# The last chunk's tail: another order of the sums, earlier stores, a separate buffer for the transposed rows, one bank copied by ScalarE

## The chip, the core and the metric

The kernel runs on one core of a Trainium2 chip. A core has TensorE (PE, matmuls into PSUM), VectorE (DVE), ScalarE (ACT) and GpSimd (POOL) for elementwise work, and SyncE (SP), which here only issues DMAs. The metric is the device time in microseconds (us); the median of several runs counts. Profiles are of one execution each.

## The reference

An FNet mixing step, then a gated feed-forward block with a sigmoid gate, in float32:

```python
X = np.fft.fft(x, axis=1)            # x: 8 x 3008 x 256
X = np.fft.fft(X, axis=2)
x2 = X.real.reshape(8 * 3008, 256)
gate = 1.0 / (1.0 + np.exp(-(x2 @ w_gate)))   # 256 x 1536
val = x2 @ w_val                              # 256 x 1536
out = (gate * val) @ w_out                    # 1536 x 256
```

The real part of a Fourier transform of real input has a symmetry: row k and row 3008 - k are made from the same two products, once with a plus and once with a minus between them. The kernel computes both rows of such a pair together; below they are called the rows k and the mirrored rows.

## The kernel before

**Tiling.** There are 8 batches. In each, the 1505 rows k are cut into six chunks, five of 252 and the last of 246. A chunk goes through the 1536 features in 12 steps of 128 features, so the main loop (line 749) has 8 x 6 x 12 = 576 iterations. An iteration does, for its 128 features: `front_a` and `front_b` (eight matmuls in the trace, into a PSUM bank called `pf`), `gate_a` and `gate_b` (two sigmoids on ScalarE and three elementwise instructions on VectorE, which give the gated values `h`), and one third of `back` for an earlier group of three steps.

**The product with w_out.** `back` (line 567) multiplies three steps' `h` with blocks of `w_out`, as a fast matrix multiplication with 15 products: 17 blocks of sums of `h` (made by GpSimd, `H_SUMS`, buffer `sf`) against 15 blocks of `w_out`. The 15 products lie in five PSUM banks `po0` to `po4`, three in a bank, and are added up over the chunk's four groups. In the fourth group, when a bank is complete, it is copied (line 584) to the SBUF tile `c`, in which product i lies at columns i*R to (i+1)*R, with R = 168, or 164 in chunks of 246. The last chunk of all doesn't copy bank 4: its products 12 to 14 are read from PSUM.

**The sums.** `finish` (line 591) combines the 15 products into the output with the list `C_SUMS` (line 66). An entry `((dst, a, b, op), e)` sets product dst to a + b or a - b. With e = 1 the entry goes to GpSimd, but in the last chunk alone; in all others every sum is VectorE's. When all is done, rows 3, 4, 5 of `c` hold one half of the output features and rows 12, 13, 14 the other (`OUT = (3, 12)`). The first n columns of each half (products 3, 4 and 12, 13) belong to the rows k, the next n (products 4, 5 and 13, 14) to the mirrored rows. `flip(s, h)` (line 610) transposes one of these four pieces on VectorE into the tile `os` (s = 0: rows k, s = 1: mirrored rows, h: which half), and `store(s)` (line 617) issues eight DMAs of it: for each of four groups of partitions one of 56 KB and one of the rest, 5 to 7 KB. In the last chunk these alternate between SP's and ScalarE's queues; otherwise all are SP's. The tile `os` has one buffer.

**What sets the order.** The order of instructions on every engine is the order in which the program issues them. In all chunks but the last, `finish` doesn't do its work at once: it appends each sum, flip and flip-with-store to the list `later`, and each iteration of the main loop takes two or three items from it (line 767: two in even iterations, three in odd ones). What is left of the list after iteration 575 is done behind the last `gate_b` (line 774), ahead of the last matmuls' copies. In the last chunk, `finish` does everything at once.

A chunk's list has 24 items: 14 sums (up to the one that sets product 5), `flip(0, 0)`, `flip(1, 0)`, six sums, then `flip(0, 1)` with `store(0)`, and `flip(1, 1)` with `store(1)`. Each DMA also waits until the DMA that had its completion semaphore before it is done; there are eight of these semaphores for the DMAs of SP and ScalarE, used in turn.

Of the kernel before, what the change touches and what calls it, by code (L numbers as in the profile page):

```python
# [7 lines left out]
F32 = mybir.dt.float32  # L8
# [54 lines left out]
            (10, 10), (14, 1), (15, 7), (16, 14))  # L63
PLACE = (0, 1, 2, 5, 3, 4, 6, 7, 8, 9, 10, 11, 14, 13, 12)

C_SUMS = (((8, 1, 8, 0), 0), ((1, 1, 0, 0), 0), ((3, 3, 1, 0), 0), ((1, 6, 2, 0), 1), ((0, 0, 10, 1), 0),
          ((11, 0, 11, 0), 1), ((4, 4, 0, 1), 0), ((4, 4, 1, 0), 0), ((11, 11, 5, 0), 1),
          ((9, 9, 8, 0), 1), ((10, 14, 8, 1), 0), ((7, 7, 10, 0), 0), ((6, 11, 6, 0), 1),
          ((5, 5, 7, 1), 0), ((9, 13, 9, 1), 0), ((9, 9, 2, 0), 0), ((14, 9, 14, 0), 0),
          ((13, 13, 6, 1), 0), ((12, 9, 12, 0), 0), ((12, 11, 12, 1), 0))  # L70
OUT = (3, 12)
HUGE = float((2 ** 24 - 1 - 2 ** 20) * 2.0 ** -7)

# [2 lines left out]
def kernel(  # L76
# [10 lines left out]
    nc = tc.nc  # L87
    B, _, _, _, D = xf.shape
    F = moe_w_gate.shape[1]
    P = 128  # L90
    S = out.shape[0] // B
    M = S // 2
    NK = M + 1
# [5 lines left out]
    CH = 252  # L99
    NB = 1 + max(b // 3 for b in PLACE)  # L100
    WC = 256
    HD = D // 2
    TB = 32
# [16 lines left out]
    sp = ctx.enter_context(tc.tile_pool(name="sp", bufs=2))  # L120
    cp = ctx.enter_context(tc.tile_pool(name="cp", bufs=2))
    op = ctx.enter_context(tc.tile_pool(name="op", bufs=1))
# [3 lines left out]
    def mm(o, l, r, start, stop):  # L126
        nc.tensor.matmul(o, l, r, start=start, stop=stop, skip_group_check=True)  # L127
# [370 lines left out]
    def seed(i):  # L498


        _, _, n, f, _ = cut(i)
        PF[i] = bank("pf").rearrange("p (g n) -> p g n", g=2)[:, :, 0:n]
        for g in range(2 if i >= NFT else 0):
            nc.scalar.activation(PF[i][:, g], EK[i // NFT], AF.Copy, scale=ge[:, g, f : f + 1])  # L504

    def front_a(i):
        (pk, *_), ks, _, _, fs = cut(i)
        if i < NFT:
            seed(i)
        for g in range(2):  # L510
            mm(PF[i][:, g], G1[:, g, fs], pk[:, ks], i < NFT and g == 0, True)

    def part(i):

        pqe, ks, n, f, _ = cut(i)
        AP[i] = app.tile([P, 2, CH], F32, name="ae", tag="ae")[:, :, 0:n]
        if i >= NFT:
            nc.scalar.activation(AP[i], PF[i], AF.Copy, scale=2.0)  # L518
            return
        for g in range(2):  # L520
            nc.vector.scalar_tensor_tensor(out=AP[i][:, g], in0=pqe[2][:, ks],  # L521
                                           scalar=ge[:, g, f : f + 1], in1=PF[i][:, g],
                                           op0=ALU.mult, op1=ALU.add)

    def front_b(i):
        (_, qk, *_), ks, _, _, fs = cut(i)
        for g in range(2):
            mm(PF[i][:, g], G2[:, g, fs], qk[:, ks], False, True)

    def gate_a(i):  # L530

        n = cut(i)[2]
        p, fh = i // 3, i % 3
        z = Z[i] = zp.tile([P, 2, CH], F32, name="z", tag="z")[:, :, 0:n]
        if fh == 0:
            H[p] = hp.tile([P, 3, 2 * WC], F32, name="h", tag="h")[:, :, 0 : 2 * n]
        nc.scalar.activation(H[p][:, fh, 0:n], PF[i][:, 0], AF.Sigmoid)  # L537
        if i < NFT:
            nc.vector.scalar_tensor_tensor(out=z[:, :, ::-1], in0=AP.pop(i), scalar=2.0, in1=PF[i],  # L539
                                           op0=ALU.mult, op1=ALU.subtract)  # L540
        else:
            nc.vector.tensor_tensor(z[:, :, ::-1], AP.pop(i), PF[i], op=ALU.subtract)  # L542

    def block(p, i):

        R = 2 * chunks[groups[p][1]][1] // 3
        return H[p][:, i % 3, i // 3 * R : (i // 3 + 1) * R] if i < 9 else SF[p][:, i - 9, 0:R]
# [16 lines left out]
    later = []  # L564
    C = {}

    def back(p, part):

        b, c, g = groups[p]
        n = chunks[c][1]  # L570
        R = 2 * n // 3
        last = p == len(groups) - 1
        if part == 0 and g == 0:
            PO[:] = [pso.tile([P, 2 * WC], F32, name=f"po{t}", tag=f"po{t}") for t in range(NB)]
        for at_, (hb, wb) in list(enumerate(PRODUCTS))[part * 5 : part * 5 + 5]:
            t, j = divmod(PLACE[at_], 3)
            mm(PO[t][:, j * R : (j + 1) * R], wf[:, g, wb], block(p, hb), g == 0 and at_ % 3 == 0,
               g == NG - 1)
            if g == NG - 1 and at_ % 3 == 2:
                if t == 0:  # L580
                    C[0] = cp.tile([P, 10 * WC], F32, name="c", tag="c")
                    nc.gpsimd.memset(C[0][:, 15 * R : 15 * R + 40], 0.0)
                if not (last and t == NB - 1):
                    (nc.vector.tensor_copy if t % 2 else nc.scalar.copy)(
                        C[0][:, 3 * t * R : 3 * (t + 1) * R], PO[t][:, 0 : 3 * R])
        if part == 2:
            del H[p], SF[p]
            if g == NG - 1:
                finish(b, c, last)

    def finish(b, c, last):
        k0, n = chunks[c]
        R = 2 * n // 3
        more = k0 + n > NK
        nb = -(-n // TB)
        t = C.pop(0)
        queues = (nc.sync, nc.scalar) if last else (nc.sync,)
        os_ = []

        new = set()  # L600

        def sum_(dst, a, b, op, engine=nc.vector):

            there = lambda i: last and i >= 3 * (NB - 1) and i not in new
            v = [PO[NB - 1][:, (i - 3 * NB + 3) * R : (i - 3 * NB + 4) * R] if there(i) else
                 t[:, i * R : (i + 1) * R] for i in (a, b)]
            engine.tensor_tensor(t[:, dst * R : (dst + 1) * R], *v, op=(ALU.subtract, ALU.add)[op])  # L607
            new.add(dst)

        def flip(s, h):  # L610
            if not os_:
                os_.append(op.tile([P, NK + 1], F32, name="os", tag="os")[:, 0 : 4 * WC].rearrange(
                    "p (s b h j) -> p s b h j", s=2, h=2, j=TB))
            c0 = OUT[h] * R + (n + more if s else 0)
            nc.vector.transpose(os_[0][:, s, 0:nb, h, :], t[:, c0 : c0 + nb * TB])

        def store(s):
            m, r0 = (min(n, M - k0), b * S + k0) if s == 0 else (
                n - (k0 == 0) - more, b * S + S - k0 - n + 1 + more)
            full = m // TB  # L620
            for a in range(4):
                ps = slice(a * TB, (a + 1) * TB)
                cs = slice(a * 2 * TB, (a + 1) * 2 * TB)
                queues[a % len(queues)].dma_start(
                    out=out[r0 : r0 + full * TB, cs].rearrange("(b t) d -> t b d", t=TB),
                    in_=os_[0][ps, s, 0:full].rearrange("p b h j -> p b (h j)"))
                if m > full * TB:
                    queues[a % len(queues)].dma_start(out=out[r0 + full * TB : r0 + m, cs],
                                      in_=os_[0][a * TB : a * TB + m - full * TB, s, full].rearrange(
                                          "p h j -> p (h j)"))  # L630

        def add(f):
            if last:
                f()
            else:
                later.append(f)
        for x, e in C_SUMS:
            add(lambda x=x, e=e: sum_(*x, engine=(nc.vector, nc.gpsimd)[last and e]))
            if x[0] == 5:
                add(lambda: flip(0, 0))  # L640
                add(lambda: flip(1, 0))
        for half in range(2):
            add(lambda half=half: (flip(half, 1), store(half)))

# [60 lines left out]
    for j in range(3, len(jobs)):  # L707
        w, c = jobs[j]
        i = (0, 1, 4, 7, 9, 10)[c] if w == 2 else 2 * c - 3 + w
# [4 lines left out]
    count = 3 * len(groups)  # L714
# [34 lines left out]
    for i in range(count):  # L749
        front_a(i)  # L750
        if i < NFT:
            part(i)
        if i:
            gate_a(i - 1)
        if i >= NFT:
            part(i)
        if i0 <= i + 1 < count:
            seed(i + 1)
        if i:
            gate_b(i - 1)  # L760
        todo = pre.pop(i, []) + use.pop(i, [])
        for f in [parts_.pop(0)] + todo if parts_ else todo + [lambda: parts_ and parts_.pop(0)()]:
            f()
        if i >= 5:
            back((i - 5) // 3, (i - 5) % 3)
        front_b(i)
        for f in later[0 : 2 + i % 2]:
            f()
        del later[0 : 2 + i % 2]
        for f in side.pop(i, []):  # L770
            f()
    gate_a(count - 1)
# [3 lines left out]
    for i in range(count, count + 5):  # L776
        back((i - 5) // 3, (i - 5) % 3)
# [49 lines left out]
```

## Time and profile before

| what | value |
|---|---|
| median of three runs | 1982.71 us (1982.51 to 1985.28) |
| the profiled execution, its own time | 1985.11 us |
| its span, first to last instruction | 1983.2 us |
| mean granted TensorE clock | 0.993 |
| PE busy | 1936.4 us, 98% of the span |
| DVE, ACT, POOL busy | 1488.3, 1338.3, 1624.8 us |
| last matmul ends | 1968.73 us |

Times inside the profile are counted from the first instruction. Lines of the profile give start, duration, engine, line of the kernel, operation and tiles; what stands in brackets is the time for which the engine was idle before, and what ended it. `SPq` and `ACTq` are DMA issues on the queues of SP and ScalarE. A group of several instructions of one kind is merged into one row with its count. A TensorE at 98% busy doesn't mean that it works at its peak, but that there is next to nothing between its matmuls.

### The profile page before, as it was taken

Reading aid. Unit: us, or ns where it says so; the run is one execution under the profiler, and the core shown is the slowest. Engines: PE = TensorE matmul, PEld = TensorE weight load, DVE = VectorE, ACT = ScalarE, POOL = GpSimd, SP = SyncE. Lnnn points to the kernel's source line nnn. Section 1 sums busy time; section 2 is a strip of 40 time slices with the busy share of each in tenths; the row PEclk is TensorE's granted clock in tenths of the full one; section 3 lists DMA queues with packets and bytes.
Section 4 is the critical chain, followed back from the end, with each engine's and each line's share of the span. In section 5 each row is a group of like instructions: output and inputs, shape, how many; then the busy total and the mean of one; then the engine's idle time right before and its main releaser. Section 6 shows DMA issues by size and latency. Waiting matters only on the chain.

```text
span 1983.2 us, 34391 instructions
## 1 busy us (share of the span) xinstructions
PE 1936.4 (98%) x11232; PEld 1790.2 (90%) x11232; DVE 1488.3 (75%) x3179; ACT 1338.3 (67%) x3102; POOL 1624.8 (82%) x2857
## 2 busy tenths in 40 slices
PE   6899999999999999999999999999999999999997
PEld 4689889998999899998999989999899989999996
DVE  7788777886787677786778867787678777777776
ACT  3467667675777667775777757777577766777774
POOL 3879898997889878997889868998688886777775
PEclk8999999999999999999999999999999999999999
DMA  8353423212112120222013121221210110011001
GB/s 266 88 132 85 124 50 104 51 22 78 18 46 54 19 77 14 54 50 77 15 21 78 20 77 20 45 54 20 77 22 14 18 23 14 14 18 23 14 16 30
DMA packets 171444, 101.41 MB, mean 51 GB/s; under 512 B 133890, under 2 KB 163204, under 8 KB 168588
## 3 DMA queue, kind: packets, MB, share of 16 engines
q1 hardware_dynamic: 169294, 98.64, 20.3%
q8 instruction: 90, 1.47, 0.3%
q10 hardware_dynamic: 1940, 0.56, 0.1%
q14 instruction: 88, 0.72, 0.1%
q0 software_dynamic: 32, 0.00, 0.0%
HBM read 74.45 MB, written 50.18 MB: 63 GB/s over the span
## 4 chain that ended last, share of the span: by engine, by line
PE 94%; DMA 2%; DVE 2%; POOL 1%; ACT 1%; issue 0%; SPq 0%; ACTq 0%; DVEq 0%; POOLq 0%
PE pf L127 48%; PE po L127 41%; PE ev L127 4%; DMA ge<-G 1%; DMA st<-in_stab_dram 1%; PE od L127 1%; PE ps L127 0%; DVE wf L315 0%; DMA wx<-in_moe_w_val_dram 0%; DVE ae L521 0%; POOL sf L560 0%; POOL wf L315 0%; DVE z L539 0%; DMA raw<-in_moe_w_gate_dram 0%; DMA wx<-in_moe_w_gate_dram 0%
## 5 line engine op out<-in xcount | busy, mean ns | idle before, releaser
L560 POOL TENSOR_TENSOR sf<-h 128x168 f32<-128x168 f32 (+1 forms) x960 | 550.8, 592 | 233.1 <-DVE h L556 233.0
L560 POOL TENSOR_TENSOR sf<-h,sf 128x168 f32<-128x168 f32 (+1 forms) x1152 | 646.1, 581 | 54.2 <-DVE h L556 54.2
L127 PE MATMUL pf<-qk,G 128*128 128x252 f32 (+1 forms) x2304 | 582.7, 376 | 3.8 <-DVE ae L521 1.9
L127 PE MATMUL pf<-pk,G 128*128 128x252 f32 (+1 forms) x2304 | 583.0, 376 | 0.0
L556 DVE TENSOR_TENSOR h<-z 128x252 f32<-128x252 f32 (+1 forms) x576 | 293.7, 510 | 377.0 <-ACT z L555 376.4
L504 ACT ACTIVATE pf<-ek,ge 128x252 f32<-128x252 f32 (+1 forms) x1128 | 531.4, 471 | 18.4
L127 PE MATMUL po<-sf,wf 128*128 128x168 f32 (+1 forms) x3072 | 530.4, 306 | 0.0
L518 ACT ACTIVATE ae<-pf 128x504 f32<-128x504 f32 (+1 forms) x564 | 332.6, 590 | 240.1 <-PE pf L127 239.3
L127 PEld LDWEIGHTS pf<-pk,G 128*128 128x128 f32 x2304 | 436.3, 190 | 53.1 <-issue 2.3
L127 PEld LDWEIGHTS po<-sf,wf 128*128 128x128 f32 x3072 | 473.3, 190 | 8.4
L127 PE MATMUL po<-h,wf 128*128 128x168 f32 (+1 forms) x2688 | 475.9, 306 | 2.1 <-ACT a L471 1.6
L607 DVE TENSOR_TENSOR c<-c 128x168 f32<-128x168 f32 (+1 forms) x950 | 467.1, 514 | 8.5
L127 PEld LDWEIGHTS po<-h,wf 128*128 128x128 f32 x2688 | 427.5, 190 | 19.2 <-ACT a L471 2.0
L127 PEld LDWEIGHTS pf<-qk,G 128*128 128x128 f32 x2304 | 409.9, 190 | 30.7 <-DVE ae L521 2.9
L542 DVE TENSOR_TENSOR z<-ae,pf 128x504 f32<-128x504 f32 (+1 forms) x564 | 372.4, 660 | 19.1 <-ACT h L537 18.8
L537 ACT ACTIVATE h<-pf 128x252 f32<-128x252 f32 (+1 forms) x576 | 218.7, 380 | 172.3 <-PE pf L127 160.2
L555 ACT ACTIVATE z<-z 128x252 f32<-128x252 f32 (+1 forms) x576 | 230.8, 401 | 76.7 <-DVE z L542 46.5
L554 DVE TENSOR_TENSOR h<-h,pf 128x252 f32<-128x252 f32 (+1 forms) x576 | 231.7, 402 | 0.0
L560 POOL TENSOR_TENSOR sf<-sf 128x168 f32<-128x168 f32 (+1 forms) x192 | 114.3, 595 | 15.1
L127 PE MATMUL ev<-st,x 63*128 63x376 f32 (+4 forms) x372 | 99.0, 418 | 8.8 <-DVE x L338 6.0
L560 POOL TENSOR_TENSOR sf<-sf,h 128x168 f32<-128x168 f32 (+1 forms) x192 | 107.5, 560 | 0.0
L127 PEld LDWEIGHTS ev<-st,x 63*128 63x128 f32 (+1 forms) x372 | 66.8, 188 | 37.0 <-issue 7.3
(115 smaller groups left out, 876.5 us busy)
## 6 DMA issues: line engine op xcount, KB each, us to landing
x<-xr SPq DMA_DIRECT2D x14, 1536.0 KB
out_dram<-os SPq DMA_DIRECT2D x380, 56.0 KB
xr<-in_xf_dram SPq DMA_DIRECT2D x14, 768.0 KB
xr<-in_xf_dram SPq DMA_DIRECT2D x35, 256.0 KB
ek<-ed SPq DMA_DIRECT2D x39, 126.0 KB
out_dram<-os SPq DMA_DIRECT2D x288, 7.0 KB
x<-in_xf_dram SPq DMA_DIRECT2D x2, 1512.0 KB
tr<-in_stab_dram SPq DMA_DIRECT2D x2, 1129.5 KB
```

Source lines behind the costliest of these rows:

```text
L127: nc.tensor.matmul(o, l, r, start=start, stop=stop, skip_group_check=True)
L504: nc.scalar.activation(PF[i][:, g], EK[i // NFT], AF.Copy, scale=ge[:, g, f : f + 1])
L518: nc.scalar.activation(AP[i], PF[i], AF.Copy, scale=2.0)
L537: nc.scalar.activation(H[p][:, fh, 0:n], PF[i][:, 0], AF.Sigmoid)
L542: nc.vector.tensor_tensor(z[:, :, ::-1], AP.pop(i), PF[i], op=ALU.subtract)
L554: nc.vector.tensor_tensor(h[:, fh, 0:n], h[:, fh, 0:n], PF.pop(i)[:, 1], op=ALU.mult)
L555: nc.scalar.activation(z[:, 0], z[:, 0], AF.Sigmoid)
L556: nc.vector.tensor_tensor(h[:, fh, n:], z[:, 0], z[:, 1], op=ALU.mult)
L560: nc.gpsimd.tensor_tensor(block(p, dst), block(p, a), block(p, b), op=(ALU.subtract, ALU.add)[op])
L607: engine.tensor_tensor(t[:, dst * R : (dst + 1) * R], *v, op=(ALU.subtract, ALU.add)[op])
```

## The change

There are four edits, three for the last chunk and its neighbour alone, one for the order of the sums everywhere.

- `C_SUMS` has a new order, and other entries go to GpSimd in the last chunk (six instead of five). The sums for products 3, 4, 12 and 13 come first, then `flip(0, 0)` and `flip(0, 1)` with `store(0)`, then products 7 and 5, product 14 (`C_LAST`), and then `flip(1, 1)` and `flip(1, 0)` with `store(1)`. This holds for all chunks; the number of sums, flips and stores is the same.
- In the last chunk the transposed rows go to a buffer of the pool that holds `sf`, instead of the one buffer of `os`.
- In the last chunk bank 3 is copied by ScalarE instead of VectorE.
- In the last eight iterations of the main loop three items of `later` are done, not two or three, so that nothing is left of the list behind the loop.

```diff
+C_SUMS = (((3, 3, 1, 0), 0), ((3, 3, 0, 1), 0), ((8, 1, 8, 0), 0), ((1, 6, 2, 0), 1), ((0, 0, 10, 1), 0),
+          ((11, 0, 11, 0), 0), ((9, 9, 8, 0), 1), ((11, 11, 5, 0), 0), ((4, 4, 0, 1), 1),
+          ((6, 11, 6, 0), 0), ((4, 4, 1, 0), 1), ((9, 13, 9, 1), 0), ((10, 14, 8, 1), 0), ((9, 9, 2, 0), 0),
+          ((12, 9, 12, 0), 0), ((12, 12, 11, 1), 0), ((13, 13, 6, 1), 0),
+          ((7, 7, 10, 0), 1), ((5, 5, 7, 1), 1))
+C_LAST = (14, 9, 14, 0)
...
-                    (nc.vector.tensor_copy if t % 2 else nc.scalar.copy)(
+                    (nc.vector.tensor_copy if t == 1 or t == 3 and not last else nc.scalar.copy)(
...
-                os_.append(op.tile([P, NK + 1], F32, name="os", tag="os")[:, 0 : 4 * WC].rearrange(
-                    "p (s b h j) -> p s b h j", s=2, h=2, j=TB))
+                full = (sp.tile([P, 8 * (2 * CH // 3)], F32, name="os", tag="sf") if last else
+                        op.tile([P, NK + 1], F32, name="os", tag="os"))
+                os_.append(full[:, 0 : 4 * WC].rearrange("p (s b h j) -> p s b h j", s=2, h=2, j=TB))
...
         for x, e in C_SUMS:
+            if x[0] == 7:
+                add(lambda: flip(0, 0))
+                add(lambda: (flip(0, 1), store(0)))
             add(lambda x=x, e=e: sum_(*x, engine=(nc.vector, nc.gpsimd)[last and e]))
-            if x[0] == 5:
-                add(lambda: flip(0, 0))
-                add(lambda: flip(1, 0))
-        for half in range(2):
-            add(lambda half=half: (flip(half, 1), store(half)))
+        add(lambda: sum_(*C_LAST))
+        add(lambda: flip(1, 1))
+        add(lambda: (flip(1, 0), store(1)))
...
-        for f in later[0 : 2 + i % 2]:
+        n = 3 if i >= count - 8 else 2 + i % 2
+        for f in later[0:n]:
             f()
-        del later[0 : 2 + i % 2]
+        del later[0:n]
```

## The prediction

> **What bounds the kernel now.** I read first the busy time by stretches, then the chain of waits from 1960 us on, then the tail engine by engine in order of time. The stretches (busy us and instruction count of PE, PEld, DVE, ACT, POOL; granted clock, DMA share, GB/s):
>
> ```profile
> 400.00:1900.00 1500.00, 1500.00 (x8832) 1400.21 (x8831) 1118.34 (x2428) 1052.84 (x2434) 1252.03 (x2231) 1.00 0.16 37
> 1950.00:1969.00 19.00, 18.73 (x120) 17.96 (x119) 15.55 (x36) 9.35 (x21) 14.17 (x28) 1.00 0.07 12
> 1969.00:1984.00 15.00, 0.00 (x0) 0.00 (x0) 6.08 (x18) 0.00 (x0) 2.78 (x5) 0.66 0.35 56
> ```
>
> From 400 to 1900 us TensorE has no idle time, so nothing that the other engines save there can shorten the run. Its last matmul ends at 1968.73; the remaining 14.5 us to 1983.2 are the tail of the last chunk, and only there can this change gain. VectorE in the tail (start, duration):
>
> ```profile
> 1967.94 0.67 DVE L584 COPY c<-po 128x492 f32<-128x492 f32 x1 [1.00 <-PE po L127]
> 1968.52 2.48 DVE L607 TENSOR_TENSOR c<-c 128x164 f32<-128x164 f32 x6
> ...
> 1970.93 0.32 DVE L607 TENSOR_TENSOR c<-po,c 128x164 f32<-128x164 f32 x1
> 1971.28 0.91 DVE L607 TENSOR_TENSOR c<-c 128x164 f32<-128x164 f32 x2
> 1973.90 0.77 DVE L615 STREAM_TRANSPOSE os<-c 128x256 f32<-128x256 f32 x2 [1.72 <-DMA out_dram<-os]
> 1974.60 0.29 DVE L607 TENSOR_TENSOR c<-po,c 128x164 f32<-128x164 f32 x1
> ...
> 1976.48 0.77 DVE L615 STREAM_TRANSPOSE os<-c 128x256 f32<-128x256 f32 x2
> ```
>
> Nine sums, then 1.72 us of standing still until the previous chunk's stores let go of the one `os` buffer, two transposes, six sums, two transposes. The chain runs through that wait:
>
> ```profile
> 1961.78 6.14 PE po L127 x44
> ...
> 1967.94 0.67 DVE c L584
> ...
> 1972.38 1.44 DMA out_dram<-os
> ...
> 1976.48 0.45 DVE os L615
> ```
>
> Then the two queues store both halves (start, duration; first and last issue of each queue's two stores):
>
> ```profile
> 1976.95 0.33 SPq L624 DMA_DIRECT2D out_dram<-os  x1
> ...
> 1978.79 0.33 SPq L624 DMA_DIRECT2D out_dram<-os  x1
> ...
> 1979.99 0.39 SPq L628 DMA_DIRECT2D out_dram<-os  x1
> ```
>
> ```profile
> 1979.12 0.35 ACTq L624 DMA_DIRECT2D out_dram<-os  x1
> ...
> 1980.33 0.36 ACTq L628 DMA_DIRECT2D out_dram<-os  x1
> ```
>
> Call T the first issue of the last chunk's first store: T = 1976.95. The last landing is at 1982.01 by the trace's semaphore events and the span ends at 1983.22: T + 6.27. So the question is how far T moves, and whether the 6.27 us behind it stay.
>
> **What the Trainium skill says.** (1) SBUF — State Buffer, "Who interferes with whom": a VectorE instruction with two SBUF inputs contends with a GpSimd instruction that reads SBUF, one with at most one SBUF input doesn't. The trace agrees: beside GpSimd's sums, a VectorE sum from SBUF alone takes 0.59 or 0.47 us instead of 0.32, the one with a PSUM input 0.32:
>
> ```profile
> 1969.84 0.59 DVE L607 TENSOR_TENSOR c<-c 128x164 f32<-128x164 f32 x1
> 1970.53 0.47 DVE L607 TENSOR_TENSOR c<-c 128x164 f32<-128x164 f32 x1
> ```
>
> (2) DMA: Bandwidth & Descriptors, "Issuing engines are not separate DMA queues": a second issuing queue saves only sequencer time. Agreed: between 1978 and 1980.5 both queues' packets keep the DMA share near its limit, and a 56 KB store that needed 1.57 us on SP's first issue needed 2.09 us on ScalarE's.
>
> **The change part by part.**
>
> *Steady state, 47 chunks.* Nineteen sums plus `C_LAST` are still 20 sums, four transposes and sixteen DMAs, in another order, all sums on VectorE. `later` still gives 2 or 3 items an iteration, so store 0 leaves two iterations sooner (item 18 instead of 22) and store 1 in the same one. VectorE is busy 1118 of 1500 us. I cost this at 0, hidden behind TensorE. Without that cover each neighbouring pair that depends on itself would cost 0.09 us (0.34 apart instead of 0.25); the new order has no more such pairs than the old.
>
> *Three items an iteration in the last eight.* Eight times 2.5 = 20 of the 24 items fitted before the end, and two sums, two transposes and both stores' issue were left over (1964.06 on; SP issued until 1972.80). Now 24 fit. Store 0 of the previous chunk issues from about 1959.4 and store 1 until 1966.4 (16 DMAs of 0.42 us on average), landing by 1968. The price is one more sum (0.34 to 0.66 us) in four iterations of 3.05 us. An iteration with three sums took VectorE 2.88 us from product to product (1959.53 to 1962.41), and two iterations hold about 1.3 us of its idle time, so it fits: 0 taken, at most 4 x 0.25 = 1 us.
>
> *A place of its own for the transposed rows.* Removes the 1.72 us wait. The `sf` buffer that it takes was last read by matmuls that end by 1964.6, so no wait takes its place. With the previous edit both remove the same wait; they are not added.
>
> *Bank 3 to ScalarE.* Its bank 2 copy ends at 1967.67, before bank 3 is ready, so the copy runs 1967.94 to 1968.51. VectorE is free from 1966.94 and does the three sums on banks 0 to 2 (1967.04 to 1968.15) while it waited before.
>
> *The order of the last chunk's sums.* Bank 3's first reader `(0,0,10)` starts at 1968.56. Behind it on VectorE, until T: five more SBUF sums, four with a PSUM input, two transposes. Six SBUF sums: `(0,0,10)`, `(11,0,11)`, `(11,11,5)`, `(6,11,6)`, `(9,9,2)`, `(12,12,11)`. GpSimd does four of its six in that time, and the two it keeps for after (rows 7 and 5) overlap too, so I take 0.45 for each SBUF sum, 0.32 for each PSUM sum. With 0.04 us between dependent ones and 0.08 less where they overlap, start by start: 1968.56, 1969.07, 1969.56, 1970.10 (two waits), 1970.50, 1970.77, 1971.02, 1971.50, 1971.86, and `(13,13,6)` 1972.22; transposes 1972.47 and 1972.84 (each 0.43 long, 0.37 apart); issue 1973.2. GpSimd is not later: it gets `(9,9,8)` done near 1969.4, needed at 1970.50, and row 4 near 1970.6, needed at 1972.47. Bounds: no contention at all (six times 0.13 less) gives 1972.5; 0.59 each (six times 0.14 more) gives 1974.0. T moves by 3.75, from 2.95 to 4.45.
>
> *Store 1.* `C_LAST` and two transposes end about 1.0 us after T. The first DMA of store 1 waits for a completion of store 0 anyway (1.84 us after T on SP, 2.17 on ScalarE, as before), so this is hidden with 0.8 us to spare; rows 5 and 7 on GpSimd end near 1972.5 and are hidden too.
>
> *One new wait.* DMAs take turns on eight completion semaphores. In the built order SP's last DMA of the previous chunk now falls behind ScalarE's first one of the last chunk, which shifts the turns: SP's very last DMA (21 rows) now waits for ScalarE's first DMA of store 1. That one issues at T + 2.17 and landed 1.73 us later, T + 3.90; SP's last then issues at about T + 3.95 instead of T + 3.04. A late 7 KB store landed 1.30 us after its issue (1972.38 to 1973.68): T + 5.25 instead of T + 5.06. Nothing is queued behind it but the end. Price 0.2 to 0.5 us; I take 0.25.
>
> Sum: 3.75 - 0.25 = 3.5 us. The profiled execution took 1985.11 us with a span of 1983.2; it becomes about 1981.6 with 1979.7. The median of the runs, 1982.71, becomes 1979.2. That is 0.18%, just inside the 0.2% (4.0 us) that a measurement of this kernel can tell from no change.
>
> **Rivals.** *More (4.0 to 5.0 us, about 1978.3).* GpSimd and VectorE miss each other, T falls to 1972.5 or below. For it: one SBUF sum of the old tail, at 1971.28, kept 0.33 us beside GpSimd. Against it: GpSimd has six sums close together between 1968.3 and 1972.5.
>
> *A wait takes the place of the old one (gain 1 to 2.5 us, about 1981).* VectorE waits for a GpSimd row or store 1 waits beyond T + 1.84. It decides once GpSimd is over 1.1 us late for `(9,9,8)`, or the second transposes over 0.8 us. Against it: both slacks are larger than one GpSimd sum (0.53 to 0.62 us).
>
> *The last eight iterations stall (gain 0 to 2.5 us).* VectorE, with three items each, falls behind the gate products and the matmuls wait. Against it: the idle time counted above.
>
> *Slower (over 1986.7).* The earlier store 0 on SP holds SP's queue: it waits in order for its transposes, and the x loads and mirrors that are issued after it start later; a batch's first matmuls wait for them. Seven batches change, so it decides above 0.5 us each (3.5 us in all), and gives 1986.7 at 1.1 us each. Against it: SP already waits for the transposes 48 times, and TensorE shows no wait on a load after 216 us.
>
> **How the numbers follow.** The 3.5 us case 0.52, of which 0.12 lies beyond 4.0 us (little contention, the new DMA wait free); more 0.34; the two lesser gains 0.10; slower 0.04. Faster by over 0.2%: 0.34 + 0.12 = 0.46; slower 0.04; within 0.2%: 0.40 + 0.10 = 0.50. Range: 1977.8 (no contention and no new wait, a gain of 4.45, and 0.4 us for the spread of the runs) to 1981.0 (a lesser gain). The runs of before lie from 1982.51 to 1985.28, so the upper end also serves a median that falls higher among them.
>
> **What would show it.** ScalarE with three copies in a row, the last at 1967.9; three VectorE sums before 1968.5; no DMA wait before transposes; SP idle from 1966.4 to T; T near 1973.2; SP's last DMA issued last of all, 0.9 us after its neighbour, behind a DMA wait; the end 6.5 us after T; TensorE still without gaps. Wrong would be: TensorE's last matmul later than 1969.2, T after 1974.0, or transposes of store 1 later than T + 1.8.

## The result

The changed kernel takes 1980.32 us in the median of 20 runs (1978.57 to 1985.18); the kernel before takes 1984.51 us in 20 runs made beside them (1982.51 to 1987.8). The ratio is 0.998, with a 95% interval from 0.9973 to 0.9987: a gain of about 4 us, 2.6 to 5.4 us by the interval, which excludes zero. The median is 1.1 us above the forecast, inside its range.

The profiled execution of the changed kernel took 1978.69 us, its span is 1976.8 us. That is 6.4 us less than the span of the profile before, but only 3.7 us of it belong to the change. The busy time by stretches of the changed kernel (PE, PEld, DVE, ACT, POOL; granted clock, DMA share, GB/s):

```profile
400.00:1900.00 1500.00, 1500.00 (x8831) 1400.08 (x8830) 1142.29 (x2426) 1052.49 (x2435) 1257.46 (x2233) 1.00 0.16 37
1950.00:1965.40 15.40, 15.39 (x101) 14.79 (x99) 11.96 (x28) 7.74 (x17) 12.82 (x26) 1.00 0.22 36
1965.40:1976.80 11.40, 0.00 (x0) 0.00 (x0) 5.13 (x15) 0.00 (x0) 2.96 (x6) 0.73 0.28 45
```

From 400 us on TensorE again has no gap, and it does the same 8831 or 8832 matmuls between 400 and 1900 us. Its last matmul ends 3.34 us earlier than before (1965.39 against 1968.73). Of this, 2.7 us lie ahead of ScalarE's first `ae` instruction (line 518, the first of the second chunk; it starts at 115.92 us before and at 113.19 us in the changed kernel), and they are not the change's: this start differs from run to run, and second profiles of the two kernels have it at 114.21 and 115.32 us. The tail behind the last matmul is now 11.42 us instead of 14.49, a gain of 3.07 us.

The other 0.6 us are the change's, and lie where nothing was forecast: in the one wait of TensorE for `ae` behind that start, at 214 us before and 211 us in the changed kernel. TensorE's waits there (total, times, longest), VectorE's sum `er` of the Fourier transform, for which ScalarE and then TensorE wait, and GpSimd's work beside it, first before, then changed:

```profile
PE pf L127 <- ACT ae L518: 1.7, 1, 1.7
211.25 1.60 DVE L421 TENSOR_TENSOR er<-a 7x376 f32<-7x376 f32 x1
210.88 1.57 POOL L341 TENSOR_TENSOR x<-x 128x512 f32<-128x512 f32 x1
```

```profile
PE pf L129 <- ACT ae L520: 1.1, 1, 1.1
208.70 0.88 DVE L423 TENSOR_TENSOR er<-a 7x376 f32<-7x376 f32 x1
209.13 1.57 POOL L343 TENSOR_TENSOR x<-x 128x512 f32<-128x512 f32 x1
```

The wait is 1.68 to 1.97 us in all four profiles with the old order of the sums, among them e4 and e5 below, and 1.06 to 1.16 us in all ten with the new one, e3 with the order alone included. In the four, one of the `er` sums begins while GpSimd's long instruction runs and takes 1.59 to 1.61 us; in the ten it has begun before, and no `er` sum there takes over 0.88 us. That the order shortens the wait is shown; that it does so by which of the two begins first is read from the traces and was not tested apart.

VectorE in the tail of the changed kernel (start, duration, then what it does; in brackets the idle time before):

```profile
1962.92 0.67 DVE L586 COPY c<-po 128x492 f32<-128x492 f32 x1 [1.72 <-PE po L129]
1963.70 1.19 DVE L609 TENSOR_TENSOR c<-c 128x164 f32<-128x164 f32 x3
1965.19 2.24 DVE L609 TENSOR_TENSOR c<-c 128x164 f32<-128x164 f32 x4 [0.31 <-ACT c L586]
1967.36 0.55 DVE L609 TENSOR_TENSOR c<-po,c 128x164 f32<-128x164 f32 x2
...
1968.79 0.32 DVE L609 TENSOR_TENSOR c<-po,c 128x164 f32<-128x164 f32 x1
1969.03 0.76 DVE L619 STREAM_TRANSPOSE os<-c 128x256 f32<-128x256 f32 x2
1969.71 0.28 DVE L609 TENSOR_TENSOR c<-c,po 128x164 f32<-128x164 f32 x1
1970.03 0.77 DVE L619 STREAM_TRANSPOSE os<-c 128x256 f32<-128x256 f32 x2
```

The three sums on banks 0 to 2 lie ahead of bank 3 (the idle 0.31 us is the wait for its copy), and no DMA wait stands ahead of the transposes. ScalarE's three copies and SP's stores (the first row is the previous chunk's last), each in order of time:

```profile
1962.09 0.57 ACT L586 COPY c<-po 128x492 f32<-128x492 f32 x1 [1.72 <-PE po L129]
1963.76 0.57 ACT L586 COPY c<-po 128x492 f32<-128x492 f32 x1 [1.10 <-PE po L129]
1964.59 0.57 ACT L586 COPY c<-po 128x492 f32<-128x492 f32 x1 [0.27 <-PE po L129]
```

```profile
1963.09 0.43 SPq L632 DMA_DIRECT2D out_dram<-os  x1
1969.81 0.32 SPq L628 DMA_DIRECT2D out_dram<-os  x1
...
1972.46 0.32 SPq L628 DMA_DIRECT2D out_dram<-os  x1
1973.90 0.29 SPq L632 DMA_DIRECT2D out_dram<-os  x1
```

T, the first issue of the last chunk's first store, is 1969.81. SP's last DMA is not issued 0.4 us after its neighbour as before, but 1.44 us after it. What SP's queue waited for in the tail (total, times, longest):

```profile
SPq L829 <- DMA out_dram<-os: 1.4, 1, 1.4
SPq L632 <- DMA out_dram<-os: 1.1, 1, 1.1
```

The second row is that issue: a wait for another store, which the kernel before did not have.

### The profile page after: what moved, and what is told of

Read it like the earlier page. It is cut to its first block, busy times and chain, and to the rows that moved or that the text cites. A ratio compares the mean times of both kernels' runs of the same rounds, so it can differ in the third digit from the quotient of the medians.

```text
span 1976.8 us, 34387 instructions
## 1 busy us (share of the span) xinstructions
PE 1932.9 (98%) x11232; PEld 1788.1 (90%) x11232; DVE 1518.7 (77%) x3177; ACT 1337.7 (68%) x3103; POOL 1631.4 (83%) x2858
## 4 chain that ended last, share of the span: by engine, by line
PE 94%; DMA 2%; DVE 2%; ACT 1%; POOL 1%; issue 0%; ACTq 0%; DVEq 0%; SPq 0%; POOLq 0%
PE pf L129 48%; PE po L129 41%; PE ev L129 4%; DMA st<-in_stab_dram 1%; DMA ge<-G 1%; PE ps L129 1%; PE od L129 1%; DVE wf L317 0%; DMA raw<-in_moe_w_val_dram 0%; DVE ae L523 0%; DVE z L541 0%; POOL sf L562 0%; DVE h L558 0%; POOL wf L317 0%; DVE c L609 0%
## 5 line engine op out<-in xcount | busy, mean ns | idle before, releaser
L562 POOL TENSOR_TENSOR sf<-h,sf 128x168 f32<-128x168 f32 (+1 forms) x1152 | 657.6, 591 | 58.7 <-DVE h L558 58.7
L558 DVE TENSOR_TENSOR h<-z 128x252 f32<-128x252 f32 (+1 forms) x576 | 301.3, 523 | 350.7 <-ACT z L557 350.1
L609 DVE TENSOR_TENSOR c<-c 128x168 f32<-128x168 f32 (+1 forms) x949 | 484.8, 542 | 5.5 <-ACT c L586 0.3
```

The costliest lines, as they stand in the source:

```text
L558: nc.vector.tensor_tensor(h[:, fh, n:], z[:, 0], z[:, 1], op=ALU.mult)
L562: nc.gpsimd.tensor_tensor(block(p, dst), block(p, a), block(p, b), op=(ALU.subtract, ALU.add)[op])
```

## The experiments

E is the end of the last matmul. The tail is T - E, the work from the last matmul to the first store, plus end - T, the two stores and what closes the program. "SP last" and "ACT last" are the last store's issue on either queue, counted from T. The last column is the time from ScalarE's first `ae` to the end: it holds the tail and the wait at 211 to 214 us. All are read from the trace, so they don't carry the spread of the first 120 us.

| run | T - E | end - T | tail | SP last | ACT last | from `ae` |
|---|---|---|---|---|---|---|
| before | 8.22 | 6.27 | 14.49 | 3.04 | 3.38 | 1867.31 |
| changed | 4.42 | 7.00 | 11.42 | 4.09 | 3.62 | 1863.62 |
| e1: no own place | 4.40 | 6.75 | 11.15 | 3.02 | 3.61 | 1863.37 |
| e2: order and bank 3 | 4.20 | 6.68 | 10.87 | 3.05 | 3.63 | 1863.16 |
| e3: order alone | 5.01 | 6.24 | 11.25 | 3.04 | 3.33 | 1863.48 |
| e4: own place alone | 6.59 | 8.01 | 14.60 | 5.36 | 3.29 | 1867.70 |
| e5: three items alone | 6.33 | 6.27 | 12.61 | 3.02 | 3.35 | 1866.17 |
| e6: changed, GpSimd's sums left out | 3.60 | 6.98 | 10.58 | 4.16 | 3.62 | 1862.84 |
| e7: changed, all sums on VectorE | 4.07 | 7.13 | 11.20 | 4.00 | 3.61 | 1863.42 |
| e8: e2 with all sums on VectorE | 4.36 | 6.71 | 11.07 | 3.03 | 3.63 | 1863.42 |
| e9: changed, again | 4.39 | 6.89 | 11.29 | 3.97 | 3.59 | 1863.58 |
| e10: before, again | 8.31 | 6.36 | 14.68 | 3.03 | 3.33 | 1867.63 |
| e11: e1 with all sums on VectorE | 4.07 | 6.79 | 10.85 | 3.04 | 3.61 | 1862.99 |
| e12: e3 and one ScalarE instruction | 5.03 | 6.57 | 11.60 | 3.04 | 3.62 | 1863.81 |

The tail of one kernel repeated within 0.2 us and T - E within 0.1 us (e9, e10), so steps of 0.3 us and more can be read from the tail. The total can't resolve them: runs of one kernel lie up to 6.9 us apart, and the one run of e1 took 1987.28 us, since its first `ae` came only at 122.03 us. From `ae` on, the two kernels lie 3.7 to 4.0 us apart, next to the 4.19 us between their medians.

**e1, the own place taken back.**

```diff
-                full = (sp.tile([P, 8 * (2 * CH // 3)], F32, name="os", tag="sf") if last else
-                        op.tile([P, NK + 1], F32, name="os", tag="os"))
+                full = op.tile([P, NK + 1], F32, name="os", tag="os")
```

> The changed kernel with its transposed rows in the one buffer of os again (three items in the last eight iterations stay). Read from the profile: E is the end of the last matmul, T the first issue of the last chunk's first store. Before: T - E 8.22, end - T 6.27, tail 14.49 us; after: 4.42, 7.00, 11.42. Theory A (the previous chunk's stores are gone by then, and the own place only shifts the turns of the completion semaphores, so that SP's last DMA waits): T - E 4.4, SP's last DMA issued at T + 3.0 without a DMA wait, end - T 6.3, tail 10.7. Rival B (the own place is what removed the wait): a DMA wait of up to 1.7 us ahead of the first transpose, T - E about 6, tail 12.3 or more.

T - E stayed at 4.40, as theory A has it: with one buffer of `os` no wait came back. SP's queue in e1, in order of time:

```profile
1981.31 0.32 SPq L627 DMA_DIRECT2D out_dram<-os  x1
1981.67 0.37 SPq L631 DMA_DIRECT2D out_dram<-os  x1
```

The last issue is again 0.36 us behind its neighbour. So the own place brings the wait on SP's queue and, in this kernel, nothing else. The end came only 0.25 us earlier, not 0.7: end - T is 6.75 where 6.3 was expected. What else was in the 7.00 is taken up with e12.

**e2, e1 with two or three items an iteration again; e3, and bank 3 on VectorE again.** The edit to e1 for e2, and the further one for e3:

```diff
-        n = 3 if i >= count - 8 else 2 + i % 2
+        n = 2 + i % 2
...
-                    (nc.vector.tensor_copy if t == 1 or t == 3 and not last else nc.scalar.copy)(
+                    (nc.vector.tensor_copy if t % 2 else nc.scalar.copy)(
```

> The changed kernel with both edits for the stores taken back (one buffer of os, two or three items an iteration); the new order and bank 3 on ScalarE stay. Theory A (the new order alone lets the previous chunk's stores leave early enough: SP would end at E + 0.2 and the last land at E + 1.1, the transpose is wanted at E + 3.6): T - E 4.4, end - T 6.3, tail 10.7. Rival B (one of the two edits is needed): a DMA wait ahead of the first transpose, T - E 5.5 to 6.1, tail 12 or more.

> As the run before, and bank 3 on VectorE again: the new order alone. Theory A (VectorE has three sums on banks 0 to 2 to do that ScalarE's copy let it do ahead of bank 3): 1.0 to 1.2 us more, T - E 5.5, end - T 6.3, tail 11.8. Rival C (bank 3 on ScalarE is worth only the copy's difference of 0.1 us): T - E 4.5, tail 10.8.

The new order alone has no DMA wait ahead of the transposes. VectorE in e3:

```profile
1967.44 0.67 DVE L586 COPY c<-po 128x492 f32<-128x492 f32 x1 [1.00 <-PE po L129]
1968.03 2.88 DVE L609 TENSOR_TENSOR c<-c 128x164 f32<-128x164 f32 x7
1970.84 0.55 DVE L609 TENSOR_TENSOR c<-po,c 128x164 f32<-128x164 f32 x2
...
1972.26 0.32 DVE L609 TENSOR_TENSOR c<-po,c 128x164 f32<-128x164 f32 x1
1972.50 0.76 DVE L618 STREAM_TRANSPOSE os<-c 128x256 f32<-128x256 f32 x2
```

Neither edit for the stores is needed, since in the new order the previous chunk's first store leaves two iterations sooner: SP was through with both at 1967.94 in e2, 3.1 us ahead of T. That is theory A. Bank 3 on ScalarE is worth 5.01 - 4.20 = 0.81 us of T - E: the three sums on banks 0 to 2 stand behind VectorE's copy here, so bank 3's first reader starts at E + 0.60, in e2 at E - 0.23, and from there to T both take 4.4 us. Expected were 1.0 to 1.2, but the three sums took 0.84 us. The new order alone makes 3.2 of the change's 3.8 us in T - E: besides the wait, two transposes and two of VectorE's sums no longer stand between the last matmul and T. Its tail of 11.25 us is as short as the changed kernel's (11.42 and 11.29), and so is its time from `ae` on: the other three edits together gain nothing that these profiles show.

**e4, the own place alone, and e5, three items alone, on the kernel before.**

```diff
-                os_.append(op.tile([P, NK + 1], F32, name="os", tag="os")[:, 0 : 4 * WC].rearrange(
+                os_.append((sp.tile([P, 8 * (2 * CH // 3)], F32, name="os", tag="sf") if last else
+                            op.tile([P, NK + 1], F32, name="os", tag="os"))[:, 0 : 4 * WC].rearrange(
```

```diff
-        for f in later[0 : 2 + i % 2]:
+        n = 3 if i >= count - 8 else 2 + i % 2
+        for f in later[0:n]:
             f()
-        del later[0 : 2 + i % 2]
+        del later[0:n]
```

> The kernel before with the own place for the last chunk's transposed rows alone. Theory A (the wait of 1.72 us goes and nothing takes its place): T - E 6.5; end - T 6.3 to 7.0, by where SP's last DMA falls in the turns of the semaphores; tail 12.8 to 13.5. Rival D (SP, which issues the previous chunk's stores until E + 4.1, holds the last stores back, or the semaphores' turns do): T - E above 7, tail 14 or more.

> The kernel before with three items in each of the last eight iterations alone. Like the own place alone it takes away what the first transpose waited for (the previous chunk's stores are then issued by E - 2 and have landed by E), but it leaves the semaphores' turns as they were. Theory A (either edit removes the wait, and only the own place brings the new wait on SP's queue): T - E 6.5, end - T 6.3, tail 12.8. Rival D (the wait at the end comes from the earlier T itself): T - E 6.5, end - T about 8, tail 14.5 like the own place alone.

Both removed the wait ahead of the transposes, and T - E fell to 6.59 and 6.33. But e5's E itself comes 0.6 us late: the last `ae` starts 9.73 us before E, in the two kernels 9.14 us before it. With three items an iteration in the old order GpSimd's last sums of `h` end later, and TensorE's weight loads wait for them:

```profile
PEld po L127 <- POOL sf L560: 0.4, 2, 0.2
```

So e5's T comes 1.3 us sooner, not 1.9. And e4's tail is not a bit shorter than before. SP's issues and waits in e4:

```profile
1974.76 0.32 SPq L625 DMA_DIRECT2D out_dram<-os  x1
1977.82 0.30 SPq L629 DMA_DIRECT2D out_dram<-os  x1
1978.21 0.32 SPq L625 DMA_DIRECT2D out_dram<-os  x1
```

```profile
SPq L629 <- DMA out_dram<-os: 2.7, 1, 2.7
SPq L625 <- DVE os L616: 2.6, 1, 2.6
```

and the waits in e5:

```profile
SPq L624 <- DVE os L615: 5.1, 1, 5.1
...
SPq L624 <- DMA out_dram<-os: 0.2, 1, 0.2
```

In e4, SP's fourth DMA of the first store stands 2.7 us: its completion semaphore was last taken by ScalarE's first DMA of the second store, which itself can't go before one of the first store has landed. That DMA of ScalarE's landed at T + 3.83, and SP's went at T + 3.85. Four DMAs of SP's are queued behind it. In e5, SP waits only for what the kernel before waited for. So in e4 the gain of 1.6 us in T was given back in full by where one DMA fell in the turns of the semaphores; rival D was right on the end of e4, theory A on its T, and e5 refutes that an earlier T is what costs.

**e6, GpSimd's six sums left out; e7, all of them on VectorE.** The edits to the changed kernel:

```diff
+            if last and e:
+                continue
             add(lambda x=x, e=e: sum_(*x, engine=(nc.vector, nc.gpsimd)[last and e]))
```

```diff
-            add(lambda x=x, e=e: sum_(*x, engine=(nc.vector, nc.gpsimd)[last and e]))
+            add(lambda x=x, e=e: sum_(*x, engine=nc.vector))
```

> The changed kernel without GpSimd's six sums in the last chunk: they are left out, so part of the last chunk's output is missing. VectorE's instructions are the same. Theory A (VectorE's sums from SBUF are longer beside GpSimd's): the four sums behind bank 3's copy take 0.33 instead of 0.49 to 0.54 us, T - E 3.65. Rival E (their length comes from their waits on each other): T - E 4.3 to 4.4.

> The changed kernel with all of the last chunk's sums on VectorE, none left out. If the run without GpSimd's sums gives T - E 3.65, four sums more before the first store, one of them in the idle time ahead of bank 3, cost 3 x 0.3: T - E 4.55, so that GpSimd's help is worth only 0.1 us; end - T 7.0 (its semaphores' turns are those of the changed kernel), tail 11.5. Rival F (GpSimd's help is worth its four sums at 0.34 us each): T - E 5.8, tail 12.8.

The four sums behind bank 3's copy, in the changed kernel 2.24 us, in e6 without GpSimd:

```profile
1966.08 1.42 DVE L609 TENSOR_TENSOR c<-c 128x164 f32<-128x164 f32 x4 [0.32 <-ACT c L586]
```

The instructions and their waits on each other are the same. Of the 0.82 us, 0.75 are the four sums themselves, 0.33 us each without GpSimd's beside them; the rest is the fourth sum's start, which no longer waits for GpSimd too. And e7:

```profile
1965.19 3.39 DVE L609 TENSOR_TENSOR c<-c 128x164 f32<-128x164 f32 x11
1968.49 0.56 DVE L609 TENSOR_TENSOR c<-po,c 128x164 f32<-128x164 f32 x2
```

Eleven sums in 3.39 us, 0.31 each. VectorE does the four more sums in 0.47 us of T - E (4.07 against 3.60), and giving them to GpSimd costs 0.82. The help of GpSimd is a loss of 0.35 us here; e8, below, is a case in which it is none. This was better than theory A's 4.55, and rival F is out: sums that don't need each other's result start 0.24 us apart, and more of them can be put between those that do.

**e8 and e11, the parts that paid, together.** e8 is e2 with e7's edit, e11 is e1 with it. e9 and e10 are the two kernels again.

> What the runs so far speak for: the new order and bank 3 on ScalarE, without the own place, without the three items an iteration, and with all of the last chunk's sums on VectorE. If each part keeps its worth: T - E 4.1, end - T 6.3 to 6.7, tail 10.4 to 10.8, 0.6 to 1.0 us below the changed kernel's 11.42 and 3.9 us below the kernel before; the medians of five may hide the smaller difference, since runs of one kernel lie up to 6 us apart. If the previous chunk's stores or the semaphores' turns come back in: a DMA wait ahead of the transposes or on SP's queue, tail 11.4 or more.

> The changed kernel once more, beside the run before: how far its tail repeats. T - E 4.4, end - T 7.0, tail 11.4, each within 0.3 us; its total within the earlier runs, 1978.6 to 1985.2.

> The kernel before once more, for its tail: T - E 8.2, end - T 6.3, tail 14.5, each within 0.3 us if the tail is steady and the difference between runs lies in the first 200 us.

> The run before the last (new order, bank 3 on ScalarE, all sums of the last chunk on VectorE, one buffer of os), with the three items an iteration again. Theory (the leftover items make GpSimd's last sums of h late, and these then lengthen VectorE's first two sums; without leftover items VectorE is done with (0,0,10) 0.3 us sooner): T - E 4.07 as with all sums on VectorE, end - T 6.7 without the new wait, tail 10.8, against 11.07 in the run with leftover items. Rival (the 0.3 us was chance): T - E 4.36, tail 11.1.

e8 came out at T - E 4.36 instead of 4.07. Its eleven sums started, relative to E, at nearly the same time but took 3.71 us. In e11 they take the 3.39 of e7 again:

```profile
1965.00 3.71 DVE L609 TENSOR_TENSOR c<-c 128x164 f32<-128x164 f32 x11
```

```profile
1967.60 3.39 DVE L609 TENSOR_TENSOR c<-c 128x164 f32<-128x164 f32 x11
```

With the leftover items (e8), GpSimd's last sum of `h` ended 0.60 us before E, without them (e7) 0.93 us, and VectorE's first sum on `c` beside it took 0.71 instead of 0.33 us. So the three items an iteration are worth 0.3 us here, for another reason than the stores. With GpSimd in the sums they are worth nothing: T - E is 4.40 in e1 with them and 4.20 in e2 without. In the same way all sums on VectorE gain 0.33 us with the three items (e1 to e11) and lose 0.16 us without them (e2 to e8): in e8 the sum taken back from GpSimd finds no idle time of VectorE ahead of bank 3, whose first reader then starts at E + 0.10 instead of E - 0.23. The two edits gain only together, and together they reach a tail of 10.85 us, 0.4 to 0.6 us below the changed kernel's but no shorter than e2's, which has neither. In total time none of this can be told: ratios to the kernel before of 0.9971 (0.996 to 0.9981) for e8, 0.998 (0.9974 to 0.9987) for e11, and 0.9974 (0.9963 to 0.9985) for the changed kernel beside e8.

**e12, one more instruction in ScalarE's stream.** Added to e3:

```diff
                 if t == 0:
+                    if last:
+                        nc.scalar.copy(table, table)
                     C[0] = cp.tile([P, 10 * WC], F32, name="c", tag="c")
```

> The new order alone, and one tiny copy more in ScalarE's stream (two elements onto themselves, ahead of bank 0's copy, so nothing waits for it). In all seven runs with bank 3 on ScalarE its last store is issued at T + 3.6, in the five without at T + 3.3 to 3.4, and end - T is 0.4 longer. Theory G (it is the one more instruction in ScalarE's stream, whatever it does): last issue T + 3.6, end - T 6.7, tail 11.7. Rival H (it is the copy of bank 3 itself, so short before the stores): T + 3.3, end - T 6.25, tail 11.25 as with the new order alone.

(The runs with bank 3 on ScalarE were eight by then, with the changed kernel's first profile.) ScalarE in e12:

```profile
1961.99 0.17 ACT L584 COPY table<-table 2x1 f32<-2x1 f32 x1
...
1974.75 0.36 ACTq L629 DMA_DIRECT2D out_dram<-os  x1
1975.42 0.28 ACTq L633 DMA_DIRECT2D out_dram<-os  x1
```

and in e3, without the tiny copy:

```profile
1976.22 0.35 ACTq L627 DMA_DIRECT2D out_dram<-os  x1
1976.61 0.35 ACTq L631 DMA_DIRECT2D out_dram<-os  x1
```

Thirteen microseconds ahead of it, a copy of two elements moves ScalarE's last store from 0.39 to 0.67 us after its neighbour, and end - T from 6.24 to 6.57. Theory G holds, as far as one run can show it: the tiny copy brings ScalarE's last issue to T + 3.62, where all runs with bank 3's copy have it (3.59 to 3.63), so that copy's work is not needed to explain it. Why one more instruction does this is open.

## Why the prediction was right, and where it was not

*The bound.* Right from 400 us on, where TensorE has no gap before or after, up to its last matmul. That the change can gain only in the tail did not follow: the stretch from 200 to 400 us was not weighed, and the new order gains 0.5 to 0.9 us there in TensorE's wait for `ae`. Elsewhere it cost nothing, though VectorE's busy time from 400 to 1900 us rose from 1118 to 1142 us: over the whole run its sums from SBUF now take 542 instead of 514 ns on average, under cover of TensorE.

*Three items an iteration.* The price of 0 was right for the changed kernel: TensorE is busy 15.39 of the last 15.40 us. In the old order it would have been 0.6 us (e5). SP was free at 1963.5 and the transposes met no wait.

*A place of its own.* The step gave the 1.72 us to this edit or to the one before. Either does remove the wait when made alone (e4, e5), but e3 shows that in the new order neither is needed. The attribution was wrong, the sum for T was not, since it counted the wait once.

*Bank 3 on ScalarE.* Right in mechanism, 0.81 us. Not seen was its price at the end, the one instruction more on ScalarE: 0.33 us in e12, and end - T of 6.68 to 6.79 in e1, e2, e8 and e11 against 6.24 to 6.36 without.

*The order of the sums.* T was to move from E + 8.22 to E + 4.47; it is at E + 4.42 and 4.39. The agreement is luck in part, for two errors cancel: the four sums behind bank 3 took 0.49 to 0.54 us beside GpSimd, not 0.45, together 0.27 us more, and the other two, which begin 0.16 and 0.07 us ahead of a sum of GpSimd's, 0.31 and 0.33, together 0.26 us less. The page "SBUF — State Buffer" of the Trainium skill, section "Who interferes with whom", was the right guide here: only the sums with both inputs in SBUF grew, and e6 shows the same sums without the neighbour.

*Store 1.* Right: its last transposes end 1.0 us after T, and it goes on at T + 1.90 and T + 2.16.

*The new DMA wait.* Right in place and in net size. ScalarE's first DMA of the second store landed at T + 4.07, and SP's last DMA, on the same semaphore, was issued at T + 4.09 (forecast 3.95). It landed at T + 5.85, not 5.25, since 1.76 us passed from its issue to its landing instead of 1.30. The 1.30 was misread: the earlier store took 1.44 us, as the chain's line at 1972.38 shows. (The 1.57 us given for SP's first 56 KB store are 1.77 in the trace as well; ScalarE's 2.08 is still longer.) But without the wait the last landing was not at T + 5.06 either, ScalarE's late last store pushed it to T + 5.68 (e1). Net, the own place costs 7.00 - 6.75 = 0.25 us here, the forecast's term.

*The sum.* The tail was to lose 3.5 us and lost 3.07 (3.2 in the second profile against the first one of before). The whole difference is end - T, 7.00 against the forecast 6.52: both last stores land late, ScalarE's at T + 5.68 and SP's at T + 5.85, and either alone would have passed the forecast's T + 5.25. The median of 1979.2 was worked out from three runs whose median, 1982.71, was 1.8 us below that of 20; a gain of 3.5 us from 1984.51 would be 1981.0, the very end of the range, and 1980.32 was measured. The 0.5 to 0.9 us outside the tail, which the sum lacks, are about what is missing between the two; that they and the low start pull opposite ways helped the number.

*The rivals.* Slower, and the stall of the last eight iterations, are out for the changed kernel by TensorE's row; e5 shows that the stall was no empty danger, 0.6 us in the old order. "A wait takes the place of the old one" did not happen in the changed kernel beyond the 0.25 us, but it was a real danger: e4 is that case, with the wait on SP's queue instead of VectorE's.

## What to carry to other kernels

When the bound engine has no gaps, the time behind its last instruction is where a change off the bound can show, and it should be read as a time of its own, from the trace: in the total, 0.3 us drown in the spread of the start. But read the bound engine's waits over the whole run before saying that it has none: a single wait outside the stretch that was looked at held 0.5 to 0.9 us of this change's gain. Before adding a buffer to remove a wait, look at what a reordering does to the same wait, and at which completion semaphore every DMA gets in the built order: a DMA whose semaphore was last taken on another queue waits for that queue's DMA to land. An elementwise helper that reads the same memory as the engine on the critical path can cost more than it takes off it, or less, by when its work begins. And edits that each remove the same wait don't add up: here the new order alone does as well as all four.

## What was not expected of the hardware

Giving four sums to GpSimd lengthened VectorE's path in the changed kernel: four VectorE sums with both inputs in SBUF took 2.24 us beside it and 1.42 us without it, while the sums taken over would have cost VectorE 0.47 us. One tiny ScalarE instruction, 13 us before, delayed ScalarE's last DMA issue by 0.3 us and the end by 0.33 us; why is open.
